# Steps of two tiles: the order of y's pieces, loads and sums of x, totals and rows within a step

## Chip, core and metric

One core of one Trainium2 chip runs the whole program. The metric is device time in microseconds (us). The kernel before was run three times: 1223.5, 1219.86 and 1218.81 us, median 1219.86. One more execution of it was profiled and took 1216.93 us.

## The reference, cut to what is computed

```python
# x: (8, 4160, 192) f32, weight: (8 heads, 7 taps)
w = softmax(weight, axis=-1)                      # per head
out = einsum('hk,bskhg->bshg', w, windows of x)   # causal, 6 zeros ahead
x = out.reshape(33280, 192)
h = x @ w_in                                      # 192 -> 1024
e = exp(h - max(h)); sm = e / (sum(e) + 1e-9)
solu = h * sm
ln = (solu - mean) / sqrt(var + 1e-6) * g_ln
return ln @ w_out                                 # 1024 -> 192
```

## The kernel before, in words

The 33280 tokens are cut into 260 tiles of 128 rows. They also form 17 chunks of 1024 to 2080 tokens, about 16 tiles each. While the tiles of chunk `ch` are computed, the convolution makes y, the input of the products, for the next chunk `c1`; x of chunk `c3`, three ahead, is loaded and summed up for its scale.

A tile runs through these stages: PE makes the up-product `ph` (L800, 1024 columns in a pair of PSUM banks), DVE takes its maximum (`emit_max`, L853), ACT the exponential e (`emit_exp`, L860), DVE multiplies h into e (`emit_mul`, L870). ACT casts the upper half of e to 16 bits (`emit_hi`, L881) and sums the squares (`emit_square`, L885), POOL makes the lower half (`emit_lo`, L896), and SP issues the DMA that transposes both into `pT` (L898). Two steps later PE makes the out-product `po` from pT (`out_half`), DVE moves it to SBUF (`emit_evac`, L969), and once the group's roots are there, a row (L1040 on DVE for even j, L1036 on ACT for odd j) scales it, and a store (L1049) writes two rows out. Each engine works its own queue in order; so does SP with its DMAs, which carry the loads of x (L162), the turns of y (`turn`, L359), the doubles of y (L372), the stores and pT.

The first 32 tiles and the last six have code of their own. Between them `two_steps(i)` runs 111 times, for i = 32 to 252, each time for two tiles a = i and b = i + 1. Up-products use three pairs of PSUM banks, named by `ring`. The number of the step in its chunk is `s`. In the odd steps (1, 3, 5, 7) PE also makes the convolution of two pieces of c1 (`fold`, into `pc`, two banks of the ring's third pair); from these, ACT writes the upper half of y (`upper`, L320) and DVE the lower half (`lower`, L329), which reads both pc and the upper. There are 13 chunks with four folds each. After a fold the next step's tile b gets the pair that held the convolution, so its up-product can't begin before the lowers have been read out. The convolution itself goes into the pair of the previous step's tile b, which is free when `emit_mul` has read it.

The scale of chunk c3 needs a maximum of x: `sum_up` reads half a load (DVE, L183); after the eighth half, ACT squares them (L224), a matmul of ones (L96, `add_up`, in the last columns of a fold's first bank) totals them across the partitions, and `run_chain` goes on with small operations, up to four in a call (L205 reads the total from PSUM, L107 to L119 and L207 make the scale, POOL finishes it in L210). Then POOL can halve x to 16 bits (L243, L247, L250, from `queue`), and the loads' buffers come free (8 of them).

Of the kernel before, what the change touches and what calls it, by code (L numbers as in the profile page):

```python
# [20 lines left out]
def kernel(  # L21
# [54 lines left out]
    act, dve, pool = nc.scalar, nc.vector, nc.gpsimd  # L76
# [14 lines left out]
    def total(parts, name, bank=None):  # L91

        n = parts.shape[1]
        if bank is None:
            bank = single(f"pt_{name}")
        nc.tensor.matmul(  # L96
            bank[:, 512 - n : 512], ones if parts.dtype == F32 else ones16, parts,
            start=True, stop=True
        )
        return bank[:, 512 - n : 512]  # L100
# [24 lines left out]
    class Chunk:  # L125
# [100 lines left out]
        def add_up(self, bank=None):  # L226
            self.tp = total(self.part[:, 0 : 2 * self.np], f"x{self.ch}", bank)
# [347 lines left out]
    for e, bank in enumerate(banks):  # L575
        for q in range(2 * per):
            j = q // 2
# [224 lines left out]
    def up_half(t, slot, k):  # L802


        if k == 0:
            t.ph = pair(slot, f"ph_{t.i}")
        else:
            behind(t.ph)
        y = [t.yT[:, j, t.off : t.off + P] for j in range(NB)]
        blocks = [(y[0], whi, 0), (y[0], wlo, 0), (y[2], whi, 0), (y[1], whi, 1)]  # L810

        def of(n, q):
            w = slice(n * 512, (n + 1) * 512)
            ops = [
                (banks_of(t)[n], lhs[q], m[q, r, w], k == 0 and j == 0, k == 1 and j == 3)
                for j, (lhs, m, r) in enumerate(blocks)
            ]
            if k == 0:
                z = y[1] if q is TOP else t.y2[:, t.off : t.off + P]
                ops.append((banks_of(t)[n], z[q], wlo[q, 1, w], False, False))  # L820
            return ops

        side_by_side(of(k, TOP), of(1 - k, BOTTOM))
# [26 lines left out]
    def emit_max(t):  # L850

        t.bias = sp.tile([P, 1], F32, name=f"sm_{t.i}", tag="sm", bufs=4)
        dve.tensor_scalar(  # L853
            t.ph, t.ph, t.cv[:, 0:1], None, ALU.mult, ALU.min, accum_out=t.bias
        )

    def emit_exp(t):
        g, grp = t.g, t.grp
        t.e = sp.tile([P, F], F32, name=f"e_{t.i}", tag="e", bufs=4)
        act.activation(  # L860
            t.e, t.ph, AF.Exp, bias=t.bias, scale=-1.0, accum_out=grp.z[:, g : g + 1]
        )
# [5 lines left out]
    def emit_mul(t):  # L868

        dve.scalar_tensor_tensor(  # L870
            t.e, t.ph, t.cv[:, 3:4], t.e, ALU.mult, ALU.mult,
            accum_out=t.grp.s1[:, t.g : t.g + 1],
        )
# [41 lines left out]
    def emit_out(t):  # L915
        t.po = single(f"po_{t.i}")
        t.wide = t.grp.n > 1 and t.i >= PAIRED

        ops, per = [], NFC // NH
        for c in range(NFC):  # L920
            hi = c // per * 2 * per + c % per
            if t.wide:
                ops.append((hi, ohl[:, c].rearrange("p a d -> p (a d)"), 2 * D))
            else:
                ops += [(hi, ohi[:, c], D), (hi, olo[:, c], D)]
            ops.append((hi + per, ohi[:, c], D))
        for j, (a, w, n) in enumerate(ops):
            nc.tensor.matmul(  # L928
                t.po[:, 0:n], t.pT[:, a, :], w, start=j == 0, stop=j == len(ops) - 1
            )  # L930
# [32 lines left out]
    def emit_evac(t):  # L963
        if t.grp.raw is None:
            t.grp.open()
        if not t.wide:
            dve.tensor_copy(t.grp.raw[:, t.g, :], t.po[:, 0:D])
        else:
            dve.tensor_reduce(  # L969
                t.grp.raw[:, t.g, :],  # L970
                t.po[:, 0 : 2 * D].rearrange("p (a d) -> p d a", a=2), AX.X, ALU.add,
            )
        (rows if t.grp.ready else t.grp.waiting).append((t.grp, t.g))
# [187 lines left out]
    queue, groups, chain, rooted, rows, stores = Queue(), {}, [], [], [], []  # L1161

    def follow(c, i):

        chain.extend(
            (c.add_up, i + 1 + (c.ch > 1)) if f is None else (f, None)
            for f in c.scale_steps()
        )

        def go():  # L1170
            c.scaled = True
            if c.exact:
                return
            for j in range(c.np):
                queue.put(c.halve_steps(j, quick=c.ch == 3), (c.ch, j))

        chain.append((go, None))

    def run_rows(i):

        for _ in range(4 if i >= NT - 6 else 2 if len(rows) > 4 else 1):
            if rows:
                g, j = rows.pop(0)
                g.row(j, act if j % 2 else dve)
# [8 lines left out]
    def run_stores():  # L1193
        while stores:
            stores.pop(0)()

    def run_chain(n):
        while chain and n > 0 and chain[0][1] is None:
            chain.pop(0)[0]()
            n -= 1  # L1200
# [21 lines left out]
    def prepare(i):  # L1222
        t = tiles[i]
        c = chunks[t.ch]
        t.yT, t.y2 = c.yT, c.y2
        t.cv = c.cvm if t.k == 0 else c.cv
        pos, n, t.g = t.slot
        if pos not in groups:
            groups[pos] = Group(pos, n)
        t.grp = groups[pos]  # L1230
        return t

    def sum_up(c, h, i):
        c.sum_squares(*h)
        if c.sums == 2 * c.np:
            c.square_peaks()
            follow(c, i)
# [455 lines left out]
    def two_steps(i):  # L1693


        a, b = prepare(i), prepare(i + 1)
        x, z = tiles[i - 5], tiles[i - 4]
        ch, s = b.ch, b.k // 2
        c1, c3 = (chunks[ch + j] if ch + j < NCH else None for j in (1, 3))

        run_stores()
        evacs = []
        if left_over:
            pa, pb, *evacs = left_over
            emit_exp(pb)
        else:
            emit_out(tiles[i - 6])
            evacs = [tiles[i - 6]]
            pa = pb = None
        for d in evacs:  # L1710
            emit_evac(d)
        if pb:
            emit_mul(pb)

        got = []
        sa, sb, sc = ring
        up_half(a, sa, 0)
        up_half(b, sb, 0)
        up_half(a, sa, 1)
        if s % 2 and c1:  # L1720
            j = s - 1
            got, half, bank = fold(c1, c1.groups()[j : j + 2], sc)
            out_half(x, z, 0, slice(0, NFC // 2))
            half(0)
            out_half(x, z, 0, slice(NFC // 2, NFC))
            half(1)
            if chain and chain[0][1] is not None and chain[0][1] <= i + 2:
                add_up(i + 2, bank)
            ring[:] = [sa, sc, sb]
        else:  # L1730
            out_half(x, z, 0)
            ring[:] = [sc, sa, sb]
        up_half(b, sb, 1)
        out_half(x, z, 1)

        def move():
            for f in moves[:1]:
                f()
            del moves[:1]

        if pa:
            emit_square(pa)
            emit_hi(pb)
            emit_lo(pa, pool)
        else:
            for q in squares:
                emit_square(q)
            squares.clear()
        for k, q in doubles:
            k.double(*q)  # L1750
        doubles.clear()
        move()
        emit_max(a)
        run_chain(4)
        emit_exp(a)
        queue.run(2.0)
        run_rows(i)
        if pb:
            emit_square(pb)
            emit_lo(pb, pool)  # L1760
        if c3 and s in (0, 2, 3, 5):
            c3.load((0, 2, 3, 5).index(s))
        move()
        if c3 and 3 <= s <= 6:
            for h in c3.halves(s - 3):
                sum_up(c3, h, i)
        for k, pc, hg in got:
            k.upper(pc, *hg)
        emit_mul(a)
        for k, pc, hg in got[:1]:  # L1770
            k.lower(pc, *hg)
        emit_hi(a)
        run_rows(i)
        run_chain(4)
        emit_max(b)
        for k, pc, hg in got[1:]:
            k.lower(pc, *hg)
        queue.run(2.0)
        if got and s in (3, 7):
            part = c1.parts[s == 7]  # L1780
            if s == 3:
                c1.open(lefts[c1.ch], chunks[ch])
            moves.extend(
                lambda blk=blk: c1.turn(blk, *part) for blk in (1, 0, 2)
            )
            moves.append(lambda: doubles.append((c1, part)))
        take_rooted()
        left_over[:] = [a, b, x, z]
# [77 lines left out]
    for i in range(4 * PAIRED, NT - 6, 2):  # L1866
        two_steps(i)
# [29 lines left out]
```

## Time and profile before

| | before |
|---|---|
| median of three runs | 1219.86 us |
| profiled execution | 1216.93 us |
| its span, first to last instruction | 1215.2 us |
| granted clock of TensorE, mean | 0.998 |
| busy share of PE, DVE, ACT, POOL | 93%, 82%, 82%, 73% |
| DMA moved, mean | 187 GB/s |

The span is what the trace shows, the execution's time includes what lies around it (1.7 us). A busy share is an average over the whole span; the waits and the timelines say what a stage waits for. A timeline's row gives the start, the length and the instruction, and in brackets the idle time of the engine before it with what ended it.

### The profile page before, as it was taken

What the parts mean: (1) busy time and instruction counts of PE and PEld (TensorE: products, weight loads), DVE (VectorE), ACT (ScalarE), POOL (GpSimd) and SP (SyncE); (2) the same over time, 40 slices, a digit from 0 to 9 for tenths busy, and PEclk for the clock granted to TensorE, in tenths of its full rate; (3) what the DMA queues carried; (4) which work ended last, traced back from release to release, by engine and by line L of the source; (5) the groups of instructions that cost most, each with busy time, mean ns of one, the idle gap of its engine ahead of it and who ended that gap; (6) DMA issues with size and microseconds to landing.
All of it is one profiled execution on the core that took longest, in us unless ns stands there. A gap on an engine that the chain in (4) does not pass through costs nothing.

```text
span 1215.2 us, 34810 instructions
## 1 busy us (share of the span) xinstructions
PE 1135.8 (93%) x13681; PEld 729.2 (60%) x13681; DVE 995.6 (82%) x2024; ACT 998.7 (82%) x1789; POOL 892.8 (73%) x711
## 2 busy tenths in 40 slices
PE   5999998999999999989999999999999999999998
PEld 3665666556565656656556566565656655656656
DVE  7888987889788888878788878887888887777777
ACT  7888886888887878878888787887878888888895
POOL 3867898788686967859697595876859678555564
PEclk9999999999999999999999999999999999999999
DMA  7999999999999999999999999999999999999988
GB/s 213 185 192 184 207 207 207 205 171 206 185 200 181 194 201 181 198 173 212 187 181 195 166 202 201 171 200 165 213 194 167 204 157 172 179 171 175 178 148 169
DMA packets 727473, 227.75 MB, mean 187 GB/s; under 512 B 651646, under 2 KB 725902, under 8 KB 727310
## 3 DMA queue, kind: packets, MB, share of 16 engines
q1 hardware_dynamic: 727310, 225.53, 100.3%
q8 instruction: 108, 1.77, 0.6%
q14 instruction: 55, 0.45, 0.1%
HBM read 33.00 MB, written 25.56 MB: 48 GB/s over the span
## 4 chain that ended last, share of the span: by engine, by line
issue 22%; DVE 19%; PE 17%; POOL 16%; ACT 14%; DMA 8%; PEld 3%; SPq 1%; ACTq 0%; DVEq 0%; POOLq 0%; PEldq 0%
DVE ph L853 10%; POOL p L896 8%; PE ph L800 6%; DMA xr<-in_x_dram 4%; DMA pT<-p 3%; ACT e L860 3%; DVE e L870 3%; ACT sq L885 3%; PE po L928 3%; PE po L800 3%; PEld L800 3%; PE ph L753 3%; DVE y L329 3%; ACT y L320 2%; POOL t L1030 2%
## 5 line engine op out<-in xcount | busy, mean ns | idle before, releaser
L896 POOL TENSOR_TENSOR p<-e,p 128x1024 f16<-128x1024 f32 x257 | 547.9, 2133 | 203.0 <-ACT p L881 200.9
L800 PE MATMUL po<-ohl,pT 64*128 64x384 f16 (+1 forms) x7104 | 490.6, 283 | 5.1 <-DMA pT<-p 4.2
L800 PE MATMUL ph<-whi,yT 64*128 64x512 f16 x2664 | 441.7, 377 | 44.6 <-DVE y L329 39.1
L800 PEld LDWEIGHTS <-pT 64*128 64x128 f16 x7104 | 348.9, 94 | 138.7 <-DMA pT<-p 7.2
L870 DVE SCALAR_TENSOR_TENSOR e<-ph,cv,e 128x1024 f32<-128x1024 f32 x248 | 317.8, 1282 | 91.9 <-ACT e L860 91.5
L860 ACT ACTIVATE e<-ph,sm 128x1024 f32<-128x1024 f32 x260 | 289.3, 1113 | 116.3 <-DVE ph L853 106.7
L800 PEld LDWEIGHTS <-yT 64*128 64x128 f16 x3774 | 198.1, 94 | 242.4 <-DVE y L329 43.7
L853 DVE TENSOR_SCALAR_CACHE_REDUCE ph<-ph,cv 128x1024 f32<-128x1024 f32 x248 | 319.5, 1290 | 12.8 <-PE ph L800 6.7
L881 ACT CAST p<-e 128x1024 f16<-128x1024 f32 x245 | 255.9, 1045 | 62.1 <-DVE e L870 61.9
L885 ACT ACTIVATE sq<-e 128x1024 f32<-128x1024 f32 x260 | 272.3, 1047 | 0.2
L800 PE MATMUL ph<-wlo,yT 64*128 64x512 f16 x1110 | 257.8, 376 | 0.0
L969 DVE TENSOR_REDUCE raw<-po 128x192 f32<-128x384 f32 x247 | 126.6, 550 | 2.7 <-PE po L928 2.0
L250 POOL TENSOR_TENSOR xs<-xr,xs 128x960 f16<-128x960 f32 (+1 forms) x56 | 107.6, 1921 | 0.7
L329 DVE SCALAR_TENSOR_TENSOR y<-pc,y 112x432 f16<-112x432 f32 (+5 forms) x140 | 72.4, 534 | 38.0 <-ACT y L320 37.4
L183 DVE TENSOR_REDUCE xa<-xr 128x1 f32<-128x384 f32 x112 | 65.0, 620 | 25.4 <-DMA xr<-in_x_dram 25.4
L800 PE MATMUL ph<-wlo,y 64*128 64x512 f16 x222 | 83.6, 376 | 0.0
L928 PE MATMUL po<-ohl,pT 128*128 128x384 f16 (+1 forms) x712 | 80.2, 269 | 3.4 <-DVE raw L969 1.4
L800 PE MATMUL pc<-xs,taps_hi 64*112 64x240 f16 (+1 forms) x832 | 70.9, 258 | 6.1 <-DVE e L870 6.1
L928 PEld LDWEIGHTS <-pT 128*128 128x128 f16 x712 | 61.7, 98 | 22.9 <-issue 4.1
L753 PE MATMUL ph<-whi,yT 128*128 128x512 f16 x216 | 58.4, 380 | 1.7 <-DVE e L870 1.7
L800 PEld LDWEIGHTS <-taps_hi 64*112 64x112 f16 x832 | 51.6, 127 | 13.1 <-issue 8.7
L247 POOL TENSOR_SCALAR xr<-xr,s 128x960 f32<-128x960 f32 (+1 forms) x56 | 57.4, 1025 | 2.8 <-ACT xs L241 0.4
(166 smaller groups left out, 976.1 us busy)
## 6 DMA issues: line engine op xcount, KB each, us to landing
out_dram<-raw SPq DMA_DIRECT2D x127, 192.0 KB, 3.3
xr<-in_x_dram SPq DMA_DIRECT2D x41, 480.0 KB, 4.6
xr<-in_x_dram SPq DMA_DIRECT2D x22, 384.0 KB, 4.2
pT<-p SPq DMA_TRANSPOSE x263, 5.1
y<-yT SPq DMA_DIRECT2D x15, 140.0 KB, 3.0
y<-yT SPq DMA_DIRECT2D x15, 126.0 KB, 3.5
yT<-y SPq DMA_TRANSPOSE x102, 3.8
raw_out<-in_moe_w_out_dram SPq DMA_DIRECT2D x1, 1536.0 KB, 12.2
```

The costliest lines, as they stand in the source:

```text
L250: (2.1 * size + 0.2, lambda: pool.tensor_tensor(xl, r, h, ALU.subtract)),
L329: dve.scalar_tensor_tensor(self.at(1, col + e, col + z, a, b), pc[:, :, e:z], self.scale(), self.at(0, col + e, col + z, a, b), ALU.mult, ...
L753: nc.tensor.matmul(bank, lhs, w[:, r, n * 512 : (n + 1) * 512], start=start and j == 0, stop=stop and j == len(ops) - 1,)
L800: nc.tensor.matmul(o, lhs, w, start=start, stop=stop)
L853: dve.tensor_scalar(t.ph, t.ph, t.cv[:, 0:1], None, ALU.mult, ALU.min, accum_out=t.bias)
L860: act.activation(t.e, t.ph, AF.Exp, bias=t.bias, scale=-1.0, accum_out=grp.z[:, g : g + 1])
L870: dve.scalar_tensor_tensor(t.e, t.ph, t.cv[:, 3:4], t.e, ALU.mult, ALU.mult, accum_out=t.grp.s1[:, t.g : t.g + 1],)
L881: act.copy(t.p16[:, :, 0, :], t.halves)
L885: act.activation(junk, t.e, AF.Square, accum_out=t.grp.s2[:, t.g : t.g + 1])
L896: eng.tensor_tensor(t.p16[:, :, 1, :], t.halves, t.p16[:, :, 0, :], ALU.subtract)
L928: nc.tensor.matmul(t.po[:, 0:n], t.pT[:, a, :], w, start=j == 0, stop=j == len(ops) - 1)
L969: dve.tensor_reduce(t.grp.raw[:, t.g, :], t.po[:, 0 : 2 * D].rearrange("p (a d) -> p d a", a=2), AX.X, ALU.add,)
```

## The change

Only `two_steps` is changed. Loads of c3 are issued at the start of a step, behind the stores, in steps 0, 1, 2 and 4 (before: in its middle, in steps 0, 2, 3 and 5). Rows are taken in one place, between the exponential of a and its multiplication, two or three of them (before: in two places, one or two each). Sums of x come one half a step in steps 1 to 7, two in step 6 (before: two a step in steps 3 to 6); the eighth half is thereby summed in step 7, and the total's matmul, made in the next fold, moves from step 7 to step 1 of the next chunk. The chain's second call stands behind the maximum of b, and the first is left out in the step that makes the total. The uppers of a fold's y stand ahead of the square of the previous b and around mul(a); both lowers directly follow mul(a), ahead of the maximum of b.

```diff
--- before.py
+++ after.py
@@ -1699,6 +1699,8 @@
         c1, c3 = (chunks[ch + j] if ch + j < NCH else None for j in (1, 3))
 
         run_stores()
+        if c3 and s in (0, 1, 2, 4):
+            c3.load((0, 1, 2, 4).index(s))
         evacs = []
         if left_over:
             pa, pb, *evacs = left_over
@@ -1712,7 +1714,7 @@
         if pb:
             emit_mul(pb)
 
-        got = []
+        got, summed = [], False
         sa, sb, sc = ring
         up_half(a, sa, 0)
         up_half(b, sb, 0)
@@ -1726,6 +1728,7 @@
             half(1)
             if chain and chain[0][1] is not None and chain[0][1] <= i + 2:
                 add_up(i + 2, bank)
+                summed = True
             ring[:] = [sa, sc, sb]
         else:
             out_half(x, z, 0)
@@ -1751,30 +1754,31 @@
         doubles.clear()
         move()
         emit_max(a)
-        run_chain(4)
         emit_exp(a)
         queue.run(2.0)
-        run_rows(i)
+        for _ in range(2 + (len(rows) > 8)):
+            if rows:
+                g, j = rows.pop(0)
+                g.row(j, act if j % 2 else dve)
+        if not summed:
+            run_chain(4)
+        if c3 and s:
+            for j in ((), (0,), (1,), (2,), (3,), (4,), (5, 6), (7,), ())[s]:
+                sum_up(c3, c3.halves(j // 2)[j % 2], i)
+        for k, pc, hg in got[:1]:
+            k.upper(pc, *hg)
+        emit_mul(a)
+        for k, pc, hg in got[1:]:
+            k.upper(pc, *hg)
+        for k, pc, hg in got:
+            k.lower(pc, *hg)
         if pb:
             emit_square(pb)
             emit_lo(pb, pool)
-        if c3 and s in (0, 2, 3, 5):
-            c3.load((0, 2, 3, 5).index(s))
         move()
-        if c3 and 3 <= s <= 6:
-            for h in c3.halves(s - 3):
-                sum_up(c3, h, i)
-        for k, pc, hg in got:
-            k.upper(pc, *hg)
-        emit_mul(a)
-        for k, pc, hg in got[:1]:
-            k.lower(pc, *hg)
         emit_hi(a)
-        run_rows(i)
+        emit_max(b)
         run_chain(4)
-        emit_max(b)
-        for k, pc, hg in got[1:]:
-            k.lower(pc, *hg)
         queue.run(2.0)
         if got and s in (3, 7):
             part = c1.parts[s == 7]
```

What that moves, in the engines' queues. DVE, the fold in step 3 of a chunk; ph is the up-product of a tile (maximum in L853), e its exponential (L870 is mul), pc the convolution, xr a load of x. Before:

```order
L853 TENSOR_SCALAR ph_2552,sm_2692<-ph_2552,cv_1063 128x1024
L1040 TENSOR_SCALAR raw_1996,t_24_1585<-raw_1996,t_24_1586 128x192
L183 TENSOR_REDUCE xa_2705<-xr_0_2209 128x1 x2
L870 SCALAR_TENSOR_TENSOR e_2694,s_32_2061<-ph_2552,cv_1063,e_2694 128x1024
L329 SCALAR_TENSOR_TENSOR y_4_0_2382<-pc_4_0_2583,y_4_0_2382 112x10x32
L329 SCALAR_TENSOR_TENSOR y_4_0_2382<-pc_4_0_2583,y_4_0_2382 112x10x16
L853 TENSOR_SCALAR ph_2563,sm_2717<-ph_2563,cv_1063 128x1024
L329 SCALAR_TENSOR_TENSOR y_4_0_2382<-pc_4_0_2583,y_4_0_2382 112x10x48
L969 TENSOR_REDUCE raw_2549<-po_2584 128x192
```

The same place after:

```order
L853 TENSOR_SCALAR ph_2551,sm_2691<-ph_2551,cv_1063 128x1024
L1040 TENSOR_SCALAR raw_1996,t_24_1585<-raw_1996,t_24_1586 128x192
L183 TENSOR_REDUCE xa_2374<-xr_1_2218 128x1
L870 SCALAR_TENSOR_TENSOR e_2693,s_32_2061<-ph_2551,cv_1063,e_2693 128x1024
L329 SCALAR_TENSOR_TENSOR y_4_0_2376<-pc_4_0_2582,y_4_0_2376 112x10x32
L329 SCALAR_TENSOR_TENSOR y_4_0_2376<-pc_4_0_2582,y_4_0_2376 112x10x16
L329 SCALAR_TENSOR_TENSOR y_4_0_2376<-pc_4_0_2582,y_4_0_2376 112x10x48
L853 TENSOR_SCALAR ph_2562,sm_2713<-ph_2562,cv_1063 128x1024
```

The last of the three lowers (L329) has come ahead of the second maximum, and one sum of x (L183) is left of two.

DVE, the fold that holds a chunk's total, which L205 reads from pc. Before, in step 7:

```order
L853 TENSOR_SCALAR ph_3211,sm_3352<-ph_3211,cv_1063 128x1024
L205 TENSOR_REDUCE xm_3191<-pc_4_10_3242 128x1
L107 TENSOR_SCALAR s_3192<-xm_3191 128x1
L108 TENSOR_SCALAR s_3192<-s_3192 128x1
L111 TENSOR_SCALAR s_3192<-s_3192 128x1
L1040 TENSOR_SCALAR raw_2549,t_32_2063<-raw_2549,t_32_2064 128x192
L870 SCALAR_TENSOR_TENSOR e_3358,s_40_2730<-ph_3211,cv_1063,e_3358 128x1024
L329 SCALAR_TENSOR_TENSOR y_4_10_3044<-pc_4_10_3242,y_4_10_3044 112x9x32
L329 SCALAR_TENSOR_TENSOR y_4_10_3044<-pc_4_10_3242,y_4_10_3044 112x9x16
L114 TENSOR_SCALAR s_3192<-s_3192 128x1
```

After, in step 1 of the next chunk:

```order
L853 TENSOR_SCALAR ph_2225,sm_2366<-ph_2225,cv_1063 128x1024
L1040 TENSOR_SCALAR raw_1510,t_16_1071<-raw_1510,t_16_1072 128x192
L183 TENSOR_REDUCE xa_2374<-xr_0_2067 128x1
L870 SCALAR_TENSOR_TENSOR e_2368,s_32_2061<-ph_2225,cv_1063,e_2368 128x1024
L329 SCALAR_TENSOR_TENSOR y_4_0_2376<-pc_0_0_2256,y_4_0_2376 112x10x48 x2
L853 TENSOR_SCALAR ph_2236,sm_2389<-ph_2236,cv_1063 128x1024
L205 TENSOR_REDUCE xm_2045<-pc_0_0_2256 128x1
L107 TENSOR_SCALAR s_2046<-xm_2045 128x1
L108 TENSOR_SCALAR s_2046<-s_2046 128x1
L111 TENSOR_SCALAR s_2046<-s_2046 128x1
```

The four small operations of the total (L205 to L111) have moved from between max(a) and mul(a) to behind max(b), and a row and a sum stand in their old place.

SP, from the last pT of a chunk on into its next (xr_0 and xr_1 are the first two of a chunk's four loads of x, yT is a turn). Before:

```order
L359 DMA_TRANSPOSE yT_4029<-y_5_10_4346 128x9x112
L898 DMA_TRANSPOSE pT_4822<-p_63_4803 128x16x128
L162 DMA xr_0_4824<-in_x_dram 128x5x192
L359 DMA_TRANSPOSE yT_4029<-y_5_10_4346 128x9x112
L1049 DMA out_dram<-raw_3856 128x2x192
L898 DMA_TRANSPOSE pT_4982<-p_64_4828 128x16x128
```

After:

```order
L162 DMA xr_0_4673<-in_x_dram 128x5x192
L898 DMA_TRANSPOSE pT_4792<-p_62_4663 128x16x128
L359 DMA_TRANSPOSE yT_4021<-y_5_10_4332 128x9x112
L898 DMA_TRANSPOSE pT_4807<-p_63_4789 128x16x128
L359 DMA_TRANSPOSE yT_4021<-y_5_10_4332 128x9x112
L1049 DMA out_dram<-raw_3852 128x2x192
L162 DMA xr_1_4820<-in_x_dram 128x5x192
L898 DMA_TRANSPOSE pT_4966<-p_64_4810 128x16x128
```

The loads xr_0 and xr_1 stand ahead of the transposes of their steps, and xr_1 comes a step sooner.

## Rows read from the trace of the kernel before

**Rows 1.** The page, busy time of each engine, share of the span, instructions.

```profile
PE 1135.8 (93%) x13681; PEld 729.2 (60%) x13681; DVE 995.6 (82%) x2024; ACT 998.7 (82%) x1789; POOL 892.8 (73%) x711
```

**Rows 2.** PE's waits: waiter, releaser, us in total, times, longest us.

```profile
PE ph L800 <- DVE y L329: 39.1, 47, 1.5
...
PE pc L800 <- DVE e L870: 6.1, 10, 0.6
PE ph L800 <- DVE e L870: 5.1, 10, 0.9
PE po L800 <- DMA pT<-p: 4.2, 3, 3.5
```

**Rows 3.** Timeline of PE, 596:645: start us, us, instruction, [idle before <- releaser].

```profile
596.45 0.38 PE L800 MATMUL ph<-whi,yT 64*128 64x512 f16 x2
...
607.97 0.38 PE L800 MATMUL ph<-whi,yT 64*128 64x512 f16 x2
...
617.14 0.38 PE L800 MATMUL ph<-whi,yT 64*128 64x512 f16 x2
...
624.94 0.38 PE L800 MATMUL ph<-whi,yT 64*128 64x512 f16 x2
...
633.98 0.38 PE L800 MATMUL ph<-whi,yT 64*128 64x512 f16 x2
...
635.97 0.39 PE L800 MATMUL ph<-whi,yT 64*128 64x512 f16 x2 [0.75 <-DVE y L329]
...
642.71 0.38 PE L800 MATMUL ph<-whi,yT 64*128 64x512 f16 x2
```

**Rows 4.** Timeline of DVE in the fold step that PE begins at 624.94.

```profile
630.86 1.28 DVE L870 SCALAR_TENSOR_TENSOR e<-ph,cv,e 128x1024 f32<-128x1024 f32 x1 [1.06 <-ACT e L860]
...
633.15 0.66 DVE L329 SCALAR_TENSOR_TENSOR y<-pc,y 112x480 f16<-112x480 f32 x1 [1.00 <-ACT y L320]
...
634.06 1.29 DVE L853 TENSOR_SCALAR_CACHE_REDUCE ph<-ph,cv 128x1024 f32<-128x1024 f32 x1
...
635.26 0.65 DVE L329 SCALAR_TENSOR_TENSOR y<-pc,y 112x480 f16<-112x480 f32 x1
```

**Rows 5.** Timeline of ACT in the same fold step.

```profile
631.07 1.05 ACT L885 ACTIVATE sq<-e 128x1024 f32<-128x1024 f32 x1
...
632.11 1.01 ACT L320 ACTIVATE y<-pc 112x480 f16<-112x480 f32 x2
```

**Rows 6.** Timeline of DVE, maxima two tiles apart in a step without a fold.

```profile
616.46 1.29 DVE L853 TENSOR_SCALAR_CACHE_REDUCE ph<-ph,cv 128x1024 f32<-128x1024 f32 x1
...
624.26 1.29 DVE L853 TENSOR_SCALAR_CACHE_REDUCE ph<-ph,cv 128x1024 f32<-128x1024 f32 x1
```

**Rows 7.** Timeline of DVE in the last two steps of a chunk.

```profile
596.30 1.01 DVE L183 TENSOR_REDUCE xa<-xr 128x1 f32<-128x384 f32 x2 [2.80 <-DMA xr<-in_x_dram]
...
605.24 0.17 DVE L205 TENSOR_REDUCE xm<-pc 128x1 f32<-128x8 f32 x1 [1.24 <-PE pc L96]
```

**Rows 8.** Timeline of SP, DMA issues from 674 on.

```profile
674.49 3.96 SPq L898 DMA_TRANSPOSE pT<-p  x1
678.50 0.59 SPq L372 DMA_DIRECT2D y<-yT  x1
```

**Rows 9.** Timeline of POOL, the lo of one tile.

```profile
669.68 2.12 POOL L896 TENSOR_TENSOR p<-e,p 128x1024 f16<-128x1024 f32 x1 [2.53 <-ACT p L881]
```

**Rows 10.** Timeline of PE, the two longest waits for pT.

```profile
194.20 3.68 PE L800 MATMUL po<-ohl,pT 64*128 64x384 f16 x30 [3.51 <-DMA pT<-p]
...
681.93 1.07 PE L800 MATMUL po<-ohl,pT 64*128 64x384 f16 x14 [0.43 <-DMA pT<-p]
```

**Rows 11.** Windows: window, length, busy by engine, PEclk, DMA share, GB/s.

```profile
190.00:194.00 4.00, 0.69 (x7) 0.13 (x3) 2.85 (x7) 3.21 (x7) 3.90 (x4) 1.00 1.10 257
194.00:198.00 4.00, 3.80 (x34) 3.47 (x36) 0.88 (x4) 1.99 (x4) 4.00 (x3) 0.57 1.09 222
```

**Rows 12.** The page, DMA queue: packets, MB, share of 16 engines.

```profile
q1 hardware_dynamic: 727310, 225.53, 100.3%
```

## Prediction

> **What bounds the kernel now.** I read the page's busy times first: PE is busy for 93% of the span, every other engine for 82% or less [rows 1]. So the loop is paced by PE, and what can be won is the time in which PE stands. The waits of PE come next [rows 2]. Of the waits inside the loop three stand out, all on PSUM banks that are still being read: in 47 places the up-product of a tile waits for a lower piece of y (L329), 39.1 us; in 10 places the convolution, and in 10 an up-product, wait for the multiplication that makes e (L870), 6.1 and 5.1 us. Data in transit (pT) costs PE only 4.2 us in three places.
>
> The third view is PE's own timeline, at the first matmul of each step [rows 3]. A step without a fold lasts 624.94 − 617.14 = 7.80 us, one with a fold 633.98 − 624.94 = 9.04. But the step right after a fold lasts 642.71 − 633.98 = 8.73, though it folds nothing: its second tile's up-product stands for 0.75 us at 635.97. The ring gives that product the pair of banks in which the convolution has just been made. A fold step that also carries a chunk's total lasts 607.97 − 596.45 = 11.52, and the step after it 617.14 − 607.97 = 9.17.
>
> Why L329 is late is in DVE's and ACT's rows of the same fold [rows 4, 5]. DVE ends mul(a) at 630.86 + 1.28 = 632.14, then stands 1.00 us until ACT's two uppers (632.11, 1.01 us for both) are there, because ACT made a square of 1.05 us first. It then does one lower, a row of the output, the maximum of b (634.06, 1.29 us), and only at 635.26 the second lower, which ends at 635.91. PE goes on at 635.97. The order on DVE and ACT makes this wait, not a lack of time: ahead of mul(a), too, DVE stands 1.06 us for the exponential.
>
> The DVE chain itself leaves little room: from max to max over two tiles it takes 624.26 − 616.46 = 7.80 us [rows 6], just PE's plain step. What is put into this serial chain (max, exponential, mul, max) is paid.
>
> **Part by part.** *Lowers ahead of max(b), uppers ahead of the square.* Uppers no longer wait behind 1.05 us of square; the second is done by about 631.07 + 1.01 = 632.1, when mul(a) ends. Both lowers then take 0.66 + 0.65, so they end near 633.4 to 633.7 instead of 635.91. PE wants the bank at about 635.97 − 0.75 = 635.2: 1.5 to 1.8 us of slack, and the wait on L329 goes. With it go the L870 waits, which are the lag of DVE behind PE that the stalls on loads and totals make (next edit).
>
> The price of a printed gap: the step after the fold is 8.73 − 7.80 = 0.93 longer for a printed 0.75, so 0.18 more than it says. For 47 + 10 + 10 places: 39.1 + 6.1 + 5.1 + 67 × 0.18 = 62.4 us. One of the 47 lies just behind the 3.51 us wait for pT at 194.20 [rows 10], which nothing here moves (the queue ahead of that transpose stays as long); about 1.6 us of it, the longest with its 0.18, is not won. Left: **60.8**.
>
> *Loads sooner, sums one half at a time, the total a step later.* These take away what DVE stood for in the last two steps of a chunk [rows 7]: 2.80 us for x in front of two sums, and 1.24 us for the total's matmul, between max(a) and mul(a). In the after order more than a whole step lies between the issue of a load and its first sum. A single sum (about 0.5 of the 1.01 for two) and one row fit into the time that DVE has for the exponential anyway (1.06 us behind a row, rows 4), so they are hidden by it; without that cover they would cost about 0.5 a step. The total's three small operations now stand behind max(b), where they delay only the evacuations. One new release comes with it: the total lies in the fold's first bank, so PE's up-product into that pair waits for L205 too, which now ends at about 632.14 + 1.31 (lowers) + 1.29 (max(b)) + 0.17 = 634.9 on the clock of rows 4, against 635.2 wanted. Below zero this can't go, since a later read frees no bank sooner; above, with 0.3 for late uppers and a little lag, 12 × 0.4 = 5. I take 1.5, near the lower end, because the estimate is ahead of PE by 0.3.
>
> *Chain length.* In a fold DVE gets 1.31 us of lowers in its chain, PE 9.04 − 7.80 = 1.24 of convolution: nearly even. Per fold 0 to 0.12 us may be left, over 52 folds (13 chunks of 4) 0 to 6.5. I take 3.5, the middle, as nothing decides. No gain is possible here beyond the waits counted already.
>
> *Rows in one place.* The same rows, two (or three) between max(a) and mul(a); even ones on DVE, odd ones on ACT. One of each kind lies under the exponential's gap. Fewer are asked for in a step when few are queued, so a row or two more stay for the end of the program: 0 to 2 us, I take 1.
>
> *The SP queue.* It carries the loads, the turns of y, the stores and pT, in order, and it is what comes next when PE is faster. POOL ends a tile's p at 669.68 + 2.12 = 671.80 [rows 9]; its transpose is issued at 674.49, 2.69 us late, and SP goes on without a gap to 679.09 [rows 8]. PE then waits 0.43 us at 681.93 [rows 10]. So the slack of pT is already nothing there, and the queue's work a chunk stays the same while the chunk's folds give up 4 × 0.93 us. A late transpose costs PE the 0.93 us by which a step is shorter, about once a chunk: 13 × 0.9 = 12. Bounds: 0, if the queue just starts sooner too, and 13 × 1.9 = 25, if two steps of each chunk are caught. I take **11**, near the middle, since rows 2 name pT only three times before.
>
> The Trainium skill (Perfetto Trace Analysis, section What "DMA-bound" means) has a rule that speaks against this change: a kernel whose issuing engine's sequencer track is solid DMA slices is bound on that sequencer. SP's track is solid in rows 8; by the rule alone no wait of PE that is taken away would shorten the loop, and the sum would be zero instead of 60.8. Rows 2 speak against it, since a queue that bounds would show as waits for pT.
>
> Sum: 60.8 − 1.5 − 3.5 − 1 − 11 = 43.8. The profiled execution took 1216.93 us (span 1215.2), the median of the runs is 1219.86, 2.9 above it. 1216.93 − 43.8 + 2.9 = **1176 us**.
>
> **Rivals.** *The queue takes most of it.* For: q1's packets fill 100.3% of the engines' span [rows 12], and SP has stretches without a gap [rows 8]. Against: in 190 to 194 the DMA moved 257 GB/s [rows 11], while 225.53 MB in 1173 us would be 192. If the transposes keep their pace in the ordinary steps, only the chunk's last fold and the step behind it gain, where DVE and PE stood and SP did not: the L870 waits, 6.1 + 5.1 + 20 × 0.18 = 14.8, and 12 × (9.17 − 7.80) = 16.4, together 31: 1189. In its strict form, SP's stream of work unchanged and everything paced by it, nothing is gained: 1220. This form is the rule of the Trainium skill named above.
>
> *The lowers still come late.* If the uppers wait for the convolution's second half, or the chain lags by half a fold, a fold and its next step keep their 9.04 + 8.73, and only the L870 waits go: 1219.9 − 14.8 = 1205. Against it: the second upper's input is there when mul(a) still runs, for ACT reads both at 632.11 without a wait.
>
> *Slower: a pT wait in every chunk.* Loads now stand ahead of transposes at the start of a chunk's first steps, beside the turns of y. At 194.20, behind such a pile, PE waited 3.51 us [rows 10], and its granted clock in that stretch was 0.57 of the full 2.4 GHz, so partly at the lower level, 1.2 [rows 11]: (1 − 0.57) × 4 = 1.7 us more. If each of 13 chunks got that, 13 × 5.2 = 68, against 60.8 − 6 = 55 of gain: 1219.9 + 13 = 1233. It decides from 4.2 us a chunk. Against it: one load at a time is moved, not a pile.
>
> **How the numbers follow.** Forecast (waits on L329 gone, pT takes some back): 0.70, its own range 1157 (no pT wait, no chain cost) to 1187 (both at their upper ends). Queue takes most: 0.12, 1189. Lowers still late: 0.06, 1205. No gain, by the strict form of the queue: 0.06, 1220. Slower: 0.06, 1233. No more than 0.2 is to be left out: 1157 to 1192 holds the first two, 0.82. A difference of 0.5% (6 us) is about what a measurement of this kernel can tell from none. Faster 0.88 (the first three), same 0.06, slower 0.06.
>
> **What the profile after would show.** Right: PE's wait for L329 falls from 39.1 us to under 5; steps after a fold last near 7.8 to 8.0; folds with a total near 9.2; no wait of DVE for x in the loop; ACT's uppers stand right behind the exponential and a row. Waits for pT of 5 to 15 us in PE's table, in steps that follow turns and loads, would bear out that term. Wrong: L329 still in PE's table with tens of us (lowers late), L205 there with over 5 (the total), or pT with over 30 (the queue). A time under 1157 would say that the chain's and the queue's terms were both too high.

## The result, and the profile after

The changed kernel took 1182.83, 1184.42 and 1186.25 us, median 1184.42, against 1219.86 before: the ratio is 0.9703 (95% interval 0.9665 to 0.9742), 35.4 us less. The prediction was 1176, 43.8 less, with 1157 to 1192 as its range. The profiled execution of after took 1186.25 us (span 1184.5), 30.7 less than that of before, so the account below is made for 30.7.

PE is busy for 95% of the span now, and the queue's packets fill a little more of the DMA engines' time than before (page, parts 1 and 3):

```profile
PE 1130.1 (95%) x13681; PEld 887.3 (75%) x13681; DVE 992.2 (84%) x2024; ACT 998.7 (84%) x1789; POOL 891.9 (75%) x711
...
q1 hardware_dynamic: 727310, 225.53, 103.8%
```

PE's waits, as in [rows 2] (waiter, releaser, us in total, times, longest us):

```profile
PE po L800 <- DMA pT<-p: 24.3, 25, 2.8
...
PE ph L800 <- DVE e L870: 4.0, 1, 4.0
...
PE ph L800 <- DVE xm L205: 0.6, 1, 0.6
```

The wait on L329, 39.1 us in 47 places, is gone. Of the 20 waits of ph and pc on L870 one is left in this table, where the loop begins. Waits for pT have come in their place, 25 instead of 3.

PE's timeline, first matmuls of the steps, of one convolution and of one second tile, as in [rows 3]; the fold begins at 587.24, the step behind it at 596.15, the fold with a total at 611.76:

```profile
587.24 0.43 PE L800 MATMUL ph<-whi,yT 64*128 64x512 f16 x2
...
591.24 0.40 PE L800 MATMUL pc<-xs,taps_hi 64*112 64x216 f16 x4
...
596.15 0.43 PE L800 MATMUL ph<-whi,yT 64*128 64x512 f16 x2
...
597.23 0.43 PE L800 MATMUL ph<-whi,yT 64*128 64x512 f16 x2
...
603.96 0.43 PE L800 MATMUL ph<-whi,yT 64*128 64x512 f16 x2
...
611.76 0.43 PE L800 MATMUL ph<-whi,yT 64*128 64x512 f16 x2
...
621.10 0.38 PE L800 MATMUL ph<-whi,yT 64*128 64x512 f16 x2
```

The step behind the fold lasts 7.81 us where it was 8.73, a step without a fold 7.80, the fold with a total 9.34 where it was 11.52. The second tile's product at 597.23 stands without a wait. The fold itself lasts 8.91 us, but that is no gain on the 9.04 of [rows 3]. Folds come in two widths, and this one has pieces of 216 columns, that of [rows 3] pieces of 240:

```profile
628.95 0.37 PE L800 MATMUL pc<-xs,taps_hi 64*112 64x240 f16 x4
```

A fold of 216 columns without a wait took 8.91 before, too (from 660.57 to 669.48), and one of 240 without a wait takes 9.04 after (from 984.31 to 993.34).

DVE in the same fold, as in [rows 4]:

```profile
592.51 0.55 DVE L183 TENSOR_REDUCE xa<-xr 128x1 f32<-128x384 f32 x1
593.65 1.28 DVE L870 SCALAR_TENSOR_TENSOR e<-ph,cv,e 128x1024 f32<-128x1024 f32 x1 [0.59 <-ACT e L860]
...
594.99 1.19 DVE L329 SCALAR_TENSOR_TENSOR y<-pc,y 112x288 f16<-112x288 f32 x3
```

And ACT, as in [rows 5]:

```profile
593.96 1.00 ACT L320 ACTIVATE y<-pc 112x288 f16<-112x288 f32 x3
594.83 1.07 ACT L885 ACTIVATE sq<-e 128x1024 f32<-128x1024 f32 x1
```

A sum of x sits under the exponential's gap, of which 0.59 us is still free. Three lowers follow mul(a) at once; they end at 596.18, 1.05 us before PE wants their bank, and the square has gone behind the uppers.

What the queue does at the start of a chunk (SP, then one row of POOL, then PE):

```profile
262.19 2.40 SPq L359 DMA_TRANSPOSE yT<-y  x1
264.69 2.11 SPq L898 DMA_TRANSPOSE pT<-p  x1
266.91 0.80 SPq L1049 DMA_DIRECT2D out_dram<-raw  x1
267.76 0.48 SPq L162 DMA_DIRECT2D xr<-in_x_dram  x1
268.34 5.21 SPq L898 DMA_TRANSPOSE pT<-p  x1
```

```profile
262.08 2.13 POOL L896 TENSOR_TENSOR p<-e,p 128x1024 f16<-128x1024 f32 x1 [2.10 <-ACT p L881]
```

```profile
276.44 1.39 PE L800 MATMUL po<-ohl,pT 64*128 64x384 f16 x14 [2.75 <-DMA pT<-p]
```

POOL has that tile's p ready at 264.21, but SP issues its transpose at 268.34, 4.1 us later, behind a turn of y, the transpose before it, a store and a load, and the issue itself takes 5.21. PE waits 2.75 us for it until 276.44, and its granted clock is 0.63 of the full 2.4 GHz in the 4 us from 276 on, so partly at the lower level, 1.2 GHz. Two shorter waits for pT, of 1.98 us until 487.23 and of 2.05 until 848.92, left it at 1.00 (windows: window, length, busy by engine, PEclk, DMA share, GB/s):

```profile
276.00:280.00 4.00, 3.56 (x38) 3.44 (x40) 1.29 (x2) 0.71 (x3) 3.91 (x4) 0.63 1.00 203
...
848.00:852.00 4.00, 3.08 (x55) 3.08 (x57) 2.29 (x7) 1.55 (x3) 2.81 (x2) 1.00 1.04 228
```

The fold with the wait of 2.75 us lasts 13.63 us, 4.59 more than without a wait; those with the other two are only 2.15 and 2.21 longer.

What has changed for pT is the delay ahead of the issue, beside PE's shorter steps. A transpose's issue on SP is as long as before (times, shortest, median and longest in ns, before and then after):

```profile
L898 SPq DMA_TRANSPOSE pT<-p x257: 1663/2729/5352, 38.0 to 1193.3; - x129
```

```profile
L898 SPq DMA_TRANSPOSE pT<-p x257: 1663/2715/5211, 38.4 to 1162.4; - x129
```

But on the mean over the loop it begins 2.03 us after POOL has the tile's p ready, and before it was 1.13.

### The profile page after: what moved, and what is told of

Same layout as the page of the kernel before. It is cut to its first block, busy times and chain, and to the rows that moved or that the text cites. A ratio compares the mean times of both kernels' runs of the same rounds, so it can differ in the third digit from the quotient of the medians.

```text
span 1184.5 us, 34794 instructions
## 1 busy us (share of the span) xinstructions
PE 1130.1 (95%) x13681; PEld 887.3 (75%) x13681; DVE 992.2 (84%) x2024; ACT 998.7 (84%) x1789; POOL 891.9 (75%) x711
## 4 chain that ended last, share of the span: by engine, by line
PE 33%; issue 17%; POOL 12%; DMA 11%; ACT 11%; DVE 9%; PEld 6%; SPq 1%; DVEq 0%; ACTq 0%; POOLq 0%; PEldq 0%
PE po L800 13%; PE ph L800 11%; DMA pT<-p 10%; POOL p L896 7%; PEld L800 6%; DVE ph L853 5%; PE pc L800 3%; ACT sq L885 3%; PE po L928 2%; PE ph L753 2%; ACT e L860 2%; ACT y L320 2%; ACT p L881 2%; DVE e L870 1%; POOL xs L250 1%
## 5 line engine op out<-in xcount | busy, mean ns | idle before, releaser
L800 PE MATMUL po<-ohl,pT 64*128 64x384 f16 (+1 forms) x7104 | 520.4, 283 | 26.4 <-DMA pT<-p 24.3
L800 PEld LDWEIGHTS <-pT 64*128 64x128 f16 x7104 | 436.2, 94 | 84.8 <-DMA pT<-p 44.4
L800 PE MATMUL ph<-whi,yT 64*128 64x512 f16 x2664 | 487.0, 377 | 4.6 <-DVE e L870 4.0
L870 DVE SCALAR_TENSOR_TENSOR e<-ph,cv,e 128x1024 f32<-128x1024 f32 x248 | 317.9, 1282 | 109.3 <-ACT e L860 108.9
L800 PEld LDWEIGHTS <-yT 64*128 64x128 f16 x3774 | 277.0, 94 | 110.5 <-DVE e L870 4.3
L853 DVE TENSOR_SCALAR_CACHE_REDUCE ph<-ph,cv 128x1024 f32<-128x1024 f32 x248 | 318.9, 1287 | 10.0 <-PE ph L800 7.3
L800 PE MATMUL ph<-wlo,yT 64*128 64x512 f16 x1110 | 300.7, 377 | 0.0
L329 DVE SCALAR_TENSOR_TENSOR y<-pc,y 112x432 f16<-112x432 f32 (+5 forms) x140 | 67.8, 532 | 27.3 <-ACT y L320 26.2
L800 PE MATMUL pc<-xs,taps_hi 64*112 64x240 f16 (+1 forms) x832 | 80.8, 259 | 0.0
L928 PEld LDWEIGHTS <-pT 128*128 128x128 f16 x712 | 61.8, 98 | 22.6 <-issue 4.3
L320 ACT ACTIVATE y<-pc 112x432 f16<-112x432 f32 (+5 forms) x140 | 57.1, 470 | 24.1 <-PE pc L800 20.7
L183 DVE TENSOR_REDUCE xa<-xr 128x1 f32<-128x384 f32 x112 | 67.8, 620 | 6.7 <-DMA xr<-in_x_dram 6.7
L800 PE MATMUL pc<-xs,taps_lo 64*112 64x240 f16 (+1 forms) x416 | 70.5, 259 | 0.0
L800 PEld LDWEIGHTS <-taps_hi 64*112 64x112 f16 x832 | 65.6, 128 | 2.2 <-issue 1.7
```

The source lines that it names most:

```text
L183: dve.tensor_reduce(self.part[:, col : col + 1], self.raw[j][:, a:z, :], AX.XY, ALU.max, apply_absolute_value=True,)
L320: act.activation(self.at(0, col + e, col + z, a, b), pc[:, :, e:z], AF.Copy, scale=self.scale(),)
L800: nc.tensor.matmul(o, lhs, w, start=start, stop=stop)
L853: dve.tensor_scalar(t.ph, t.ph, t.cv[:, 0:1], None, ALU.mult, ALU.min, accum_out=t.bias)
L870: dve.scalar_tensor_tensor(t.e, t.ph, t.cv[:, 3:4], t.e, ALU.mult, ALU.mult, accum_out=t.grp.s1[:, t.g : t.g + 1],)
L928: nc.tensor.matmul(t.po[:, 0:n], t.pT[:, a, :], w, start=j == 0, stop=j == len(ops) - 1)
```

## Experiments

Each was timed beside the kernel before on one chip, and its ratio is to that kernel there. Where loop steps are compared, a step runs from its first up-product on PE to that of the next step; these lengths were summed from PE's timelines.

**The y order alone (e1), and the rest alone (e2).** e1 is the kernel before with this part only:

```diff
         run_rows(i)
-        if pb:
-            emit_square(pb)
-            emit_lo(pb, pool)
-        if c3 and s in (0, 2, 3, 5):
-            c3.load((0, 2, 3, 5).index(s))
-        move()
...
-        for k, pc, hg in got:
+        for k, pc, hg in got[:1]:
             k.upper(pc, *hg)
         emit_mul(a)
-        for k, pc, hg in got[:1]:
+        for k, pc, hg in got[1:]:
+            k.upper(pc, *hg)
+        for k, pc, hg in got:
             k.lower(pc, *hg)
+        if pb:
+            emit_square(pb)
+            emit_lo(pb, pool)
+        if c3 and s in (0, 2, 3, 5):
+            c3.load((0, 2, 3, 5).index(s))
+        move()
         emit_hi(a)
...
         emit_max(b)
-        for k, pc, hg in got[1:]:
-            k.lower(pc, *hg)
```

> The kernel before with one part of the change alone: uppers around mul(a), both lowers between mul(a) and max(b); loads, sums, total and rows as before. Theory (the waits on L329 come from the order of y's pieces alone): PE's waits for L329, 39.1 us in 47 places, fall under 3 us; the 11 us of waits on L870 stay, since loads and totals stall DVE as before; pT takes back 3 to 10 us. Time 1176 to 1188 us. Rival (the SP queue takes the gain wherever PE is faster, whatever the loads do): waits for pT above 20 us and a time of 1195 us or more.

e2 is the changed kernel with these lines of y put back in their old order.

> The changed kernel with the old order of y's pieces: uppers behind the square, one lower behind mul(a), the other behind max(b); loads, sums, total and rows as changed. Theory: the waits on L329 are back with 35 to 45 us, the waits on L870 stay away, pT waits fall under 8 us since PE leaves the queue time again; 1205 to 1215 us. Rival (the waits for pT come from the loads' new places alone): pT keeps 20 us or more beside L329, 1220 us or more.

Measured: e1 1220.93 us, ratio 1.0012 (0.9991 to 1.0033), no change at all: the theory missed the time by over 30 us, and the rival's wait for pT of over 20 us didn't come either; e2 1197.17, ratio 0.9815 (0.9789 to 0.984), better than expected, with 27.8 us of waits on L329 where 35 to 45 were expected. The profiled execution of e1 took 1227.93 us, 7 above its median. PE's waits in e1, and DVE's for x:

```profile
PE ph L800 <- DVE e L870: 26.3, 11, 3.8
PE po L800 <- DMA pT<-p: 17.8, 16, 5.9
PE pc L800 <- DVE e L870: 10.0, 19, 0.6
```

```profile
DVE xa L183 <- DMA xr<-in_x_dram: 43.1, 11, 5.7
```

and in e2:

```profile
PE ph L800 <- DVE y L329: 27.8, 36, 1.9
...
PE po L800 <- DMA pT<-p: 5.8, 8, 1.5
```

So the y order does what it says: in e1 no up-product of the loop waits on L329 any more. But nothing is won, because the loads now come too late. In e1, DVE's wait for x grew from 25.4 us to 43.1 in the same 11 places, and PE's wait on the multiplication behind it to 26.3. One chunk's end in e1, by SP, DVE, PE and the windows:

```profile
596.92 0.96 SPq L162 DMA_DIRECT2D xr<-in_x_dram  x1
```

```profile
597.44 0.08 DVE L1040 DVE_READ_ACCUMULATOR raw<-raw,t 128x1 f32 x1
602.73 1.01 DVE L183 TENSOR_REDUCE xa<-xr 128x1 f32<-128x384 f32 x2 [5.21 <-DMA xr<-in_x_dram]
```

```profile
605.00 0.61 PE L800 MATMUL ph<-whi,yT 64*128 64x512 f16 x2 [3.76 <-DVE e L870]
```

```profile
604.00:608.00 4.00, 3.00 (x16) 1.06 (x18) 3.54 (x9) 3.74 (x7) 1.90 (x1) 0.50 1.06 233
608.00:612.00 4.00, 4.00 (x52) 2.57 (x50) 2.43 (x4) 3.13 (x5) 1.91 (x2) 0.74 0.75 154
```

The load is issued at 596.92, DVE has nothing else to do from 597.52 on and stands until 602.73. PE stands 3.76 us, and then runs at a granted clock of 0.50 for 4 us and at 0.74 for the next 4, partly or wholly at 1.2 GHz in place of 2.4. The mean granted clock of e1 is 0.987 against 0.998 before: about 0.011 × 1226 = 13 us of PE's time, at most. Summed over the loop, the 52 steps behind a fold are 35.7 us shorter than before (425.1 for 460.8), but the 12 folds with a total are 27.5 longer (156.9 for 129.4) and the 40 other folds 19.5 (379.5 for 360.0). Of pT's 17.8 us 13.0 lie in the steps behind a fold, whose gain would be larger without them.

**The y order with early loads (e8).** Is it the loads that took the gain in e1? e8 is e1 with one more edit:

```diff
         run_stores()
+        if c3 and s in (0, 1, 2, 4):
+            c3.load((0, 1, 2, 4).index(s))
...
-        if c3 and s in (0, 2, 3, 5):
-            c3.load((0, 2, 3, 5).index(s))
```

> The kernel before with the new order of y's pieces, which alone changed nothing (1220.93 us), and the loads at the start of steps 0, 1, 2 and 4; sums two a step in steps 3 to 6, total in step 7, rows in two places, all as before. Theory (the gain of the y order was given back because DVE stood 43.1 us for x in front of mul(a), and PE 26.3 us behind it): the waits for x fall under 8 us, PE's L870 under 6 us outside of the total's step, time 1186 to 1197 us; the total's wait (L205 on L96, 20 us) stays. Rival (another cause, the queue or the chain with two sums and the extra lowers in one step): 1208 us or more.

Measured: 1199.17 us, ratio 0.9814 (0.9781 to 0.9848), just above the theory's range. DVE's wait for x and the 26.3 us of PE behind it are gone; of the waits that stay, two rows:

```profile
PE po L800 <- DMA pT<-p: 28.3, 21, 6.8
...
DVE xm L205 <- PE pc L96: 17.7, 13, 2.2
```

So the early loads turn the 0 of e1 into 22 us. How these divide between loads and y order e8 can't say, since the early loads weren't run with the old order of y and nothing else; e2, which has them with sums, total and rows, gains about as much without the new order. What the new order of y adds to these is seen between e2 (ratio 0.9815) and the full change (0.9703), whose intervals lie apart: 0.0112 of 1220, about 14 us. What is left from e8 to the full change (1187.46 us in e5, the changed kernel timed again beside e8) are the total's wait on L96 and waits for pT, up to 6.8 us long here; which of sums, total and rows gives how much of these 12 us wasn't tried apart.

**Where do the waits for pT come from? Order in the queue (e3, e4).** The first piece of the diff is e3 alone, the second e4 alone; `moves` holds a part's turns and its double.

```diff
-        if c3 and s in (0, 1, 2, 4):
-            c3.load((0, 1, 2, 4).index(s))
+        if c3 and s in (0, 2, 3, 5):
+            c3.load((0, 2, 3, 5).index(s))
...
-        move()
+        if len(moves) == 1:
+            move()
         emit_hi(a)
```

> The changed kernel with the four loads of a chunk at the start of steps 0, 2, 3 and 5 in place of 0, 1, 2 and 4, nothing else. Theory A (the waits for pT, 24.3 us, come from the heap of three loads, three turns, a double and stores ahead of the transposes in steps 0 to 2): the delay of a transpose in the SP queue in the first tiles of a chunk falls from 3.5 to 4.7 us to under 3, pT waits fall to 5 to 12 us, time 1166 to 1176 us. Theory B (the queue's total work in a chunk is what counts, not its order): pT waits stay at 20 to 28 us, time 1181 to 1187 us.

> The changed kernel with one turn of y a step (in steps 0, 1, 2 and 4, 5, 6) in place of two and one, so that the double comes a step later; loads as changed. Theory A (a heap in steps 0 and 1): the first transposes of a chunk come sooner, those of step 2 later, pT waits fall to 14 to 20 us, time 1175 to 1182 us. Theory B (total work): 1181 to 1187 us, pT at 20 to 28 us.

Measured: e3 1183.84 us, from 1175.34 to 1186.94, ratio 0.9695 (0.965 to 0.974); e4 1179.54, ratio 0.9672 (0.9641 to 0.9702). PE's waits, e3 and then e4:

```profile
PE po L800 <- DMA pT<-p: 20.6, 23, 2.1
```

```profile
PE po L800 <- DMA pT<-p: 17.2, 20, 2.6
PE ph L800 <- DMA y<-yT: 6.9, 7, 1.5
```

Theory A said 5 to 12 us of pT for e3 and 1166 to 1176 us: it is 20.6, in the profile of its fastest run, and both figures lie in theory B's ranges. Those of e4 lie in theory A's. Sorted by the step in which they lie, 19 of the changed kernel's 25 waits, 21.9 us, are in steps 2 and 3, behind the turns of steps 0 and 1. In e3 these steps have 6 (6.8 us), but steps 6 and 7, behind the turns of steps 4 and 5 and the load that now stands in step 5, have 14 (10.6 us), where there were 4 (1.8 us). So the waits follow the heap, and the loads' new places only made another one. e4 took pT to 17.2, but PE now waits 6.9 us for the double of y. Neither run can be told from the changed kernel by its interval. So the order in SP's queue sets where PE waits; for how much, these two don't tell.

**Order or transport (e6, e7, e9).** In e6 the loop's loads go through ACT's queue, behind the square of the previous a.

```diff
-        def load(self, j):
-            q = nc.sync
+        def load(self, j, q=nc.sync):
...
         run_stores()
-        if c3 and s in (0, 1, 2, 4):
-            c3.load((0, 1, 2, 4).index(s))
...
             for q in squares:
                 emit_square(q)
             squares.clear()
+        if c3 and s in (0, 1, 2, 4):
+            c3.load((0, 1, 2, 4).index(s), nc.scalar)
```

e7 has the same, and the stores move to that place and queue:

```diff
-            nc.sync.dma_start(
+            (nc.scalar if via else nc.sync).dma_start(
...
-        run_stores()
...
+        via.append(1)
+        run_stores()
+        via.clear()
         if c3 and s in (0, 1, 2, 4):
```

e9 is the changed kernel with this:

```diff
+        if i > 4 * PAIRED + 8:
+            stores.clear()
         run_stores()
```

> The changed kernel itself, beside the next three on one chip, as their yardstick: 1181 to 1188 us, pT waits 20 to 28 us.

> The changed kernel with the loads of the loop issued on ACT's queue, behind the square of the previous a, in place of SP's. Theory A (pT is late because SP's issue stream is nearly solid and in order): SP is spared 41 loads, 20 us of the 833 us it is busy in the loop, three of them in the crowded steps 0 to 2; pT waits fall to 12 to 20 us, 1176 to 1182 us. Theory C (the DMA engines' own throughput holds pT, whoever issues): pT waits stay at 20 to 28 us, 1182 to 1188 us.

> As the kernel before it in this call, and the stores of the loop on ACT's queue too, ahead of the load. SP is spared 20 + 75 = 95 us of 833. Theory A: pT waits fall under 8 us, time 1162 to 1174 us, unless ACT, which pays about 0.7 us a store, holds the exponentials. Theory C: pT waits stay at 18 to 28 us, 1180 to 1190 us.

> The changed kernel with the stores of the loop left out (all from the sixth step on), so that most of the output is not written; the rest is unchanged. It measures what the DMA traffic beside pT costs. Theory C (transport: the transposes share the DMA engines with whatever else is under way, whoever issues it): the issue time of a transpose falls from 2.76 us, its landing too, pT waits fall under 5 us, time 1153 to 1165 us. Theory A' (order in SP's queue only): the issue time of a transpose stays at 2.7 to 2.8 us, only the delay ahead of it falls; pT waits 5 to 14 us, 1165 to 1178 us. Rival (pT is late by POOL and ACT, not by DMA): no change, pT at 20 us or more, 1181 us or more.

Measured: e5 1187.46 us, ratio 0.9723 (0.9684 to 0.9761); e6 1178.08, 0.9641 (0.9611 to 0.9671); e7 1209.97, 0.9892 (0.9868 to 0.9917); e9, timed with e10 to e12, 1169.38, 0.9613 (0.9581 to 0.9644). PE's waits for pT, and the transposes' issue on SP (times, shortest, median and longest in ns), in e5, e6, e7 and e9:

```profile
PE po L800 <- DMA pT<-p: 27.7, 27, 2.7
...
L898 SPq DMA_TRANSPOSE pT<-p x257: 1663/2731/5092, 37.3 to 1160.0; - x129
```

```profile
PE po L799 <- DMA pT<-p: 16.8, 19, 2.1
...
L897 SPq DMA_TRANSPOSE pT<-p x257: 1666/2818/5094, 36.8 to 1155.2; - x129
```

```profile
PE po L799 <- DMA pT<-p: 37.3, 32, 3.8
...
L897 SPq DMA_TRANSPOSE pT<-p x257: 1657/3017/6584, 38.0 to 1187.6; - x129
```

```profile
PE po L800 <- DMA pT<-p: 11.7, 13, 1.8
...
L898 SPq DMA_TRANSPOSE pT<-p x257: 1657/2538/5086, 37.0 to 1144.8; - x129
```

The stores show that a transpose's own length counts, too. SP is spared 112 of them in e7, and a transpose is issued a little sooner behind its p (1.83 us on the mean over the loop, 2.02 in e5), but it takes longer, 3.02 us at the median for 2.73, and pT costs PE 37.3 us. With the stores left out (e9) a transpose takes 2.54 and is issued 1.21 us behind its p, and pT costs 11.7. So the length of a transpose on SP is no fixed price of issuing, and theory A, for which SP's own stream was all, falls for the stores.

What lengthens a transpose can be read by sorting those of the loop by which other DMAs were under way, issued and not yet landed (one whose landing the trace doesn't tell counts until its issue ends). In e5 the median is 3.60 us beside a load (40 transposes), 2.49 beside a store and no load (59) and 2.50 beside neither (122). In e7 it is 3.08 beside a store and no load (100) and 2.26 beside neither (50). So transposes beside a load are the long ones in e5, and those beside a store only where the stores have ACT's queue. This sorts traces by what went on at the time; it is not an experiment.

Of the 26 us by which e7's loop is longer than e5's in the profiles, about 19 lie in steps that wait for pT, and most of the rest in steps that wait for the multiplication (L869). In that ACT may have its part, since DVE waits 137.2 us for exponentials there and 117.3 in e5; this wasn't tried apart. e6, where the loads moved by the same means and pT fell from 27.7 to 16.8, bears theory A out for the loads: a transpose is issued 1.76 us behind its p there, and is no shorter. e9 fell between its two theories: its time and its wait for pT lie in the ranges of A', but the transposes got shorter, as C alone had it. Order and transport both have a part; how large each is, these runs don't tell. Of the 11.7 us left in e9 10.1 lie in steps 1 to 3, where loads and turns still stand together.

**Putting together what helped (e10 to e12).** e12 is e6 with the turns of e4; e10 is e6 with the loads' steps of e3; e11 has all three.

> The changed kernel with the loads on ACT's queue in steps 0, 1, 2 and 4 and one turn of y a step. 1170 to 1178 us if the gains of both add up (9 and 5 us), 1177 to 1182 us if they are the same gain.

> The changed kernel with the loads on ACT's queue (as in the run that gave 1178 us) and in steps 0, 2, 3 and 5. If heap and order at the chunk's start still matter once the loads are off SP: pT waits under 12 us, 1170 to 1176 us. If not: 1176 to 1182 us.

> The same with one turn of y a step. If the heap matters: pT waits under 10 us, 1167 to 1175 us; against it the later double, on which PE waited 6.9 us when the turns were spread alone: then 1175 to 1182 us.

Measured: e12 1172.37 us, ratio 0.9631 (0.9611 to 0.9651); e10 1177.85, 0.9667 (0.9644 to 0.969); e11 1179.68, 0.9689 (0.9667 to 0.9712). PE in e12:

```profile
PE po L799 <- DMA pT<-p: 10.4, 9, 2.6
...
PE ph L799 <- DMA y<-yT: 6.2, 6, 1.9
```

e12 has the lowest time of all whose work is complete, 46 us under the kernel before in its own comparison (1218.41). The interval of its ratio lies below both of the changed kernel's (0.9665 to 0.9742 and, in e5, 0.9684 to 0.9761), so it beats that too, by about 9 us; from e6 it can't be told apart, so that the gains of loads and turns add up isn't shown. Loads at 0, 2, 3 and 5 gain nothing on ACT's queue either: e10 can't be told from e6, with 22.8 us of waits for pT, and e11 is slower than e12 beyond their intervals, since PE waits 13.8 us for the double of y in it.

## Why the prediction was right, and where its sizes were off

The direction, the mechanism and what is late next came as forecast, and the time lies in the range, 8 us above the point. One term makes the difference.

- *How it is measured.* The lengths of PE's steps tell it best, against what a step of its kind takes without a wait: 7.80 us without a fold, 8.91 or 9.04 with one. What goes beyond that is called its excess.
- *Gain.* The steps with a wait on L329 had about 48.4 us of excess before, and none waits on it now. The 12 folds with a total had 22.3 and have 10.5. Together 60.2 are won, where 60.8 stood. Of the 10.5 that are left, 4.5 lie in the first of these folds, behind a wait of DVE for the loop's first load:

```profile
189.34 0.55 DVE L183 TENSOR_REDUCE xa<-xr 128x1 f32<-128x384 f32 x1 [6.73 <-DMA xr<-in_x_dram]
```

So the sign "no wait of DVE for x in the loop" failed in this one place. The wait for pT of 3.51 us at 194.20, which the prediction held fixed [rows 10], is gone; the other took its place.
- *pT.* This is the mis-sized term: 11 was taken, 0 to 25 was the range. The steps that wait for pT (folds with a total left out, they are counted above) have 29.8 us of excess where they had 5.7: 24.1 more, the upper end. What was off is "about once a chunk": it was nearly twice, 25 times in 13 chunks, and 19 of these lie in the two steps that follow the chunk's first fold, as the bound's upper end had it. The clock is a small part of the 24.1: it fell behind one of these waits (0.63 at 276 to 280), about 2 us.
- *Chain.* 3.5 was taken. The 26 folds after without a total and without a printed wait for pT have 3.4 us of excess, where such folds had none before. Most of it is a wait too short for the table. In the third fold of most chunks, which takes about 9.2 us for 8.91, the convolution begins just when the multiplication of the previous b ends, at 791.33 + 1.28 = 792.61:

```profile
791.33 1.28 DVE L870 SCALAR_TENSOR_TENSOR e<-ph,cv,e 128x1024 f32<-128x1024 f32 x1 [0.46 <-ACT e L860]
...
792.68 0.39 PE L800 MATMUL pc<-xs,taps_hi 64*112 64x216 f16 x4
```

In e2, with the old order of y, the folds without a wait have 0.1 us of excess. So the lag comes with the new order.
- *Total and tail.* 1.5 and 1 were taken. L205 holds PE once, and that step has 2.1 us of excess. What follows the start of the loop's last step is no longer than before, 48.8 us for 49.5. The slack of the lowers, 1.5 to 1.8 us in the working, is 1.05 in the fold shown.
- *The sum.* 60.2 − 24.1 − 3.4 − 2.1 and 0.5 of other steps make 31.1, by which the loop is shorter; what lies around it is 0.5 longer, so that 30.6 of the span remain. Only pT's term missed by more than 2 us.
- *The range.* The ends of the forecast's own range don't follow from its terms: without a wait for pT and without a chain cost 1176 − 11 − 3.5 gives 1161, not 1157, and both at their upper ends 1176 + 14 + 3 gives 1193, not 1187. The measured 1184.42 lies within either.
- *The rivals.* "Queue takes most", 1189, was nearer to the time than the forecast's 1176; its form was wrong, since the steps behind ordinary folds did gain (7.81) and the queue took from the start of the chunk instead. The strict form, 1220 us and nothing won, is refuted by the result. The Trainium skill (Perfetto Trace Analysis, section What "DMA-bound" means) names solid DMA slices on the issuing engine's track as the mark of a DMA-bound kernel that its sequencer holds. Here SP was issuing for 85% of the loop before and for 89% after, so the mark stands in stretches only, and in e7, where SP was given less to issue, the time rose. "Lowers still late" did not come true.
- *What the prediction didn't see.* It priced the edits one by one and added them: 47.6 for y, 14.8 for loads and total. The runs show 0 for y alone (e1), 22.6 for the rest alone (e2: 1219.81 − 1197.17), and 35 for both. So the parts don't add up one by one: the new order of y gains nothing alone and about 14 us on top of the rest (0.9815 to 0.9703), since it pays only when the next deadline, here that of x's loads, moves with it.

## What to carry to other kernels

A wait that is taken away moves every deadline behind it nearer: ask of each transfer that was just in time what it does when the step is shorter, and change the two together, or a right edit shows no gain. Read a queue from when a transfer is issued and lands behind its producer, not from how solid its track is. A wait of PE can cost more than itself: look at the granted clock behind it, which fell after 2.75 us here and not after 1.98 or 2.05. The length alone doesn't decide: in e1 it fell after a wait of 2.30 us (until 455.26) and not after one of 2.57 (until 762.26). And compare a step only with one that has the same work in it.

## What the hardware showed that was not expected

A transpose's issue on SP took 2.54 us at the median with the loop's stores left out, 2.73 with the stores in the same queue and 3.02 with the same stores on ACT's queue. Moving stores and loads to ACT's queue made the time longer (1209.97 for 1187.46), moving the loads alone made it shorter (1178.08). And a stall of 3.76 us on PE was followed by 4 us at a granted clock of 0.50 and 4 at 0.74; in that program, with 26.3 us of such waits and one of 5.9 us for pT, the mean clock was 0.987 for 0.998, about 13 us of PE's time by estimate.
